# Four moves in the opening of a Fourier-mixing and feed-forward kernel on one core

## The chip, the core and the metric

The kernel runs on one core of a Trainium2 chip. A core has a matrix engine (TensorE, PE in the profile), a vector engine (VectorE, DVE), a scalar engine (ScalarE, ACT), a general engine (GpSimd, POOL) and a sync engine (SP) that here only starts transfers. The engines run their own instruction queues in order and wait for each other through semaphores. The metric is the time of one execution in device microseconds (us); lower is better. A group "PEld" in the profile is the loading of weights into TensorE, which overlaps its matmuls.

## What is computed

The reference, cut to what matters:

```python
# x: (8, 3008, 256), w_in: (256, 2048), w_out: (2048, 256), all float
X = np.fft.fft(x, axis=1)
X = np.fft.fft(X, axis=2)
x2 = X.real.astype(np.float32).reshape(8 * 3008, 256)
h = x2 @ w_in
g = h * (1.0 / (1.0 + np.exp(-1.702 * h)))
return (g @ w_out).astype(np.float32)
```

So eight batches are Fourier-transformed along the sequence (3008 = 47 x 64) and along the 256 columns, and the real part goes through a feed-forward layer of width 2048 with a sigmoid gelu. The weights arrive as 64-bit floats. [...] the kernel itself rounds them, in eight chunks (four of w_in, four of w_out), from the high and the low 32-bit word of each number.

## The kernel before

The kernel is a software pipeline over 8 batches x 6 half blocks x 8 pairs of hidden tiles. Step t of that pipeline computes the hidden activations of step t (`hidden`, `rows`, `activate`) and multiplies those of step t - 3 with w_out (`product`). The column transform is folded into w_in: a rounded chunk `wst` is multiplied by a small cosine and sine table (`fold_w`), and the results `wcs` are the weights of `hidden`. The sequence transform of batch b + 1 runs between the steps of batch b. What has nothing to hide behind is the opening: the sequence transform of batch 0 and the rounding and folding of the first weight chunks.

First the transform of batch 0. `xt` holds 32 slots of 256 columns, eight groups of four. `fold_first` adds and subtracts mirrored columns into a separate tile (`room`), with the two columns that have no mirror copied by GpSimd; `mix_first` multiplies pairs of slots into one bank of PSUM, and ScalarE copies the bank back into `xt`; `spill_first` writes it to DRAM (`Td`), from where `fill` reads it back in another layout.

```python
    def fold_first(g):

        t, e = xt[0:2 * NA, 4 * g:4 * g + 4, :], room[g][0:2 * NA]
        nc.gpsimd.tensor_copy(free(e, 0, [D, 4], [H, 2]), free(t, 0, [D, 4], [H, 2]))
        for at, op in ((1, ALU.add), (H + 1, ALU.subtract)):
            nc.vector.tensor_tensor(e[:, :, at:at + H - 1], t[:, :, 1:H], free(t, D - 1, [D, 4], [-1, H - 1]), op=op)

    def mix_first(i):

        ps, ns = bank("ps1"), (2 * i + 2, 2 * i + 1) if i < 7 else (0, 15)
        for at, n in enumerate(ns):
            for even in range(2):
                c0, c1 = (0, H + 1) if even else (H + 1, D)
                o = ps[:, at * D + c0:at * D + c1]
                for k, slot in enumerate((n, NJ - n if n else 16)):
                    rhs = room[slot // 4][:, slot % 4, c0:c1]
                    w = free(pair[:, even, slot], 0, [1, 128])
                    nc.tensor.matmul(o, lhsT=w, rhs=rhs, start=(k == 0), stop=(k == 1))
        nc.scalar.copy(xt[:, 30 - 2 * i:32 - 2 * i, :].rearrange("p j d -> p (j d)"), ps[:])

    def spill_first(lo, hi):
        for c, eng in enumerate((nc.sync, nc.scalar)):
            eng.dma_start(out=view(Td[0], (16 * c + lo - 16) * D, [NJ * D, NM], [1, (hi - lo) * D]),
                          in_=xt[NM * c:NM * c + NM, lo:hi, :].rearrange("p q d -> p (q d)"))
```

A chunk of the weights is rounded by three engines: a clamp on GpSimd, a square and two conversions of the low word on ScalarE (the square on VectorE for the first two chunks), three operations on VectorE, and an integer addition on GpSimd that ends it.

```python
    def bounds(key, first=False):


        hi, lo = raw[key][:, :, 1].bitcast(F32), raw[key][:, :, 0]
        g = sp.tile([128, 1024], F32, tag="s", bufs=3, name="g")
        m = cv.tile([128, 1024], F32, tag="m", bufs=2, name="m")
        r = cv.tile([128, 1024], U32, tag="r", bufs=2, name="r")
        nc.gpsimd.tensor_scalar(m[:], hi, scalar1=TOP, scalar2=-TOP, op0=ALU.min, op1=ALU.max)

        if first:
            nc.vector.tensor_tensor(g[:], hi, hi, op=ALU.mult)
        else:
            nc.scalar.activation(g[:], hi, ACTF.Square)
        nc.scalar.activation(r[:].bitcast(F32), lo, ACTF.Copy, scale=2.0 ** -29, bias=2.0 ** 23)
        nc.scalar.activation(r[:], r[:].bitcast(F32), ACTF.Copy, bias=-2.0 ** 23)
        pre[key] = g, m, r

    def rounded(outs, key):


    def rounded(outs, key):
        # ... (a = a tile of 128 x 1024 words; m is masked in place)
        dve.scalar_tensor_tensor(m[:], g[:], LOW * LOW, m[:], op0=ALU.is_ge, op1=ALU.mult)
        dve.tensor_scalar(a[:], bits, scalar1=3, scalar2=0x3FFFFFF8, op0=ALU.logical_shift_left, op1=ALU.bitwise_and)
        dve.scalar_tensor_tensor(a[:], bits, 0xC0000000, a[:], op0=ALU.bitwise_and, op1=ALU.bitwise_or)

        def finish():
            for out, part in outs(a[:], r[:]):
                nc.gpsimd.tensor_tensor(out.bitcast(U32), *part, op=ALU.add)
        return finish
```

`fold_w` with its last part, the `psf` matmuls that make the scalars `af2`:

```python
    def fold_w(n):
        for cs in range(2):
            ps = bank("psw")
            for i in range(2):
                nc.tensor.matmul(ps[:], lhsT=cd[:, i, cs, :], rhs=wst[n][:, i, :], start=(i == 0), stop=(i == 1))

            nc.scalar.copy(wcs[cs][:, n * 512:(n + 1) * 512].rearrange("p (f c) -> p f c", f=4),
                           free(ps[:], 0, [1, 4], [4, 128]))

        ps = bank("psf")
        for f in range(4 * n, 4 * n + 4):
            nc.tensor.matmul(ps[:, f:f + 1], lhsT=wcs[1][0:1, f * 128:f * 128 + 128], rhs=twos[:], start=True, stop=True)
        nc.scalar.copy(af2[:, 4 * n:4 * n + 4], ps[:, 4 * n:4 * n + 4])
```

The second stage of the sequence transform (`rotate` mends one column, `stage2` multiplies, VectorE transposes) and the first hidden tiles:

```python
    def rotate(b, a0=0, a1=NG, copy=None):

        col = t4t[b][:, a0:a1, H]
        ps = bank("psr")
        nc.tensor.matmul(ps[:, 0:a1 - a0], lhsT=rot, rhs=col, start=True, stop=True)
        (copy or nc.vector.tensor_copy)(col, ps[:, 0:a1 - a0])
    # ... stage2: 64 small matmuls t4 -> ps, then
        for cs in range(2):
            for u in range(NU):

                nc.vector.transpose(free(pq[:], cs * 512 + u * RUN, [256, 2], [NU * RUN, 4], [1, RUN]),
                                    free(ps[u][:], cs * 256, [128, 2], [32, 4], [1, 32]))
    # ... hidden(t): four matmuls wcs, pq -> pa, pb, then ScalarE copies pa to v
    # ... rows(t): VectorE, h = v + pb; dif = nb * af2 - pb (twice); h' = pa + dif
    # ... bank(): one of four PSUM banks in turn, for pa, pb, psw, psf, psn and warm
```

The opening itself, in program order:

```python
    nc.sync.dma_start(out=w0, in_=tab1[:, 0:n0 + 4])
    for part in ((0, 4), (28, 32), (4, 8), (24, 28), (8, 16), (16, 24)):
        load_first(*part)
    load_in(0, nc.sync)
    nc.sync.dma_start(out=small[:], in_=tab2)
    load_in(1, nc.sync)
    warm(7)

    nc.scalar.copy(af2[0:1, 0:1], ones[0:1, 0:1])
    matrices()
    for i, need in enumerate(((0, 7), (1,), (6,), (2,), (5,), (3,), (4,), ())):
        for g in need:
            fold_first(g)
        mix_first(i)
        if i == 2:
            specials()
        if i == 3:
            spill_first(24, 32)
            load_out(0, nc.sync)
        if i == 5:
            spill_first(20, 24)
    spill_first(16, 20)
    fill(0, 0, 4)
    load_in(2, nc.sync)
    load_out(1, nc.sync)
    for c in range(2):
        bounds(("in", c), True)
        round_in(c)
        finish_in(c)
    fold_w(0)
    warm(3)
    bounds(("out", 0))
    round_out(0)
    finish_out(0)
    rotate(0, 0, 4)
    stage2(0, 0)
    # ...
    ahead = [("in", 2), ("out", 1), ("in", 3), ("out", 2), ("out", 3)]
    at(0, bounds, ahead[0])
    for t, (kind, c) in enumerate(ahead):
        at(t, round_out if kind == "out" else round_in, c)
        if t + 1 < len(ahead):
            at(t, bounds, ahead[t + 1])
        at(t + 1, finish_out if kind == "out" else finish_in, c)
    early[0], early[2], early[4] = 1, 2, 3
    at(1, fill, 0, 4, NG)
    for t, load, c in ((0, load_in, 3), (1, load_out, 2), (2, load_out, 3)):
        at(t, load, c, nc.sync)
    # ...
    for t in range(n + LAG):
        if t < n:
            hidden(t)
        if t == 0:
            nyquist(0, 0)
        if t >= LAG:
            product(t - LAG)
        if t in early:
            fold_w(early[t])

        if 0 < t <= n:
            activate(t - 1)
            sums(t - 1, nc.gpsimd)
        sums(t - 2, nc.vector)
        if t < n:
            rows(t)
        if t >= LAG:
            combine(t - LAG)
        for fn, args in extra.get(t, ()):
            fn(*args)
```

`warm` is a run of matmuls whose results nobody reads.

## Time and profile before

| what | us |
|---|---|
| time, median of 3 runs | 1940.95 (1939.94 to 1941.74) |
| span of the profiled execution | 1946.2 |
| PE busy in the span | 1920.2 (99%) |
| PE busy from 100 us to 1900 us | 1800 of 1800 |
| VectorE, ScalarE, GpSimd busy in the span | 1415.1, 672.5, 767.1 |
| first matmul of `product` (line 520) | 81.68 |

Times in a profile count from the start of the span. Each row of the timeline has the start, the duration, the engine, the line of the kernel, the operation, its output and input, and the number of instructions merged; in brackets stands how long the engine sat idle before it and what released it. "PEclk" is the clock that TensorE was granted, as a share of full speed. A busy PE may be a slow PE: at half clock each matmul takes twice as long and still counts as busy. A float32 matmul appears as two records.

### The profile page before, as it was taken

To read this page: it belongs to the slowest core of one execution; us is meant where nothing else is said; L and a number is where in the kernel's file an instruction comes from. 1 tells how busy PE (TensorE), PEld (TensorE's weight loads), DVE (VectorE), ACT (ScalarE), POOL (GpSimd) and SP (SyncE) were. 2 spreads that over 40 slices of the span, in tenths; PEclk is the share of its full clock that TensorE was granted. 3 is DMA by queue.
4 is the path that set the end of the run, shared out by engine and by line. 5 is a ranking of instruction groups with operands and counts; after the bars stand their busy time and mean duration, and the time that the engine had idled before them with its cause. 6 is when DMAs were issued, how large, how long until landed. Compare 5 with 4: busy or idle time off the path is not lost.

```text
span 1946.2 us, 29330 instructions
## 1 busy us (share of the span) xinstructions
PE 1920.2 (99%) x10722; PEld 1681.4 (86%) x10722; DVE 1415.1 (73%) x2935; ACT 672.5 (35%) x922; POOL 767.1 (39%) x1062
## 2 busy tenths in 40 slices
PE   7899999999999999999999999999999999999998
PEld 5598888988889888898888888898888988889887
DVE  5567777777768777777678777777777777777776
ACT  3533333333333333333333333333333333333332
POOL 4356323643235432453225622255223643233332
PEclk8899999999999999999999999999999999999999
DMA  8630352218202272034521263221721213202201
GB/s 252 178 56 11 82 86 17 49 43 123 17 12 49 54 112 18 11 58 68 89 17 37 33 107 50 28 49 42 107 31 14 18 43 60 17 12 26 18 12 22
DMA packets 144560, 103.54 MB, mean 53 GB/s; under 512 B 104706, under 2 KB 127522, under 8 KB 142944
## 3 DMA queue, kind: packets, MB, share of 16 engines
q1 hardware_dynamic: 143136, 100.62, 31.0%
q8 instruction: 85, 1.39, 0.3%
q10 hardware_dynamic: 1280, 1.05, 0.2%
q14 instruction: 59, 0.48, 0.1%
HBM read 58.38 MB, written 48.01 MB: 55 GB/s over the span
## 4 chain that ended last, share of the span: by engine, by line
PE 98%; ACT 1%; DVE 0%; DMA 0%; POOL 0%; issue 0%; SPq 0%; ACTq 0%; DVEq 0%
PE po L520 59%; PE pa L453 17%; PE pb L453 17%; PE ps L213 1%; PE ps L318 1%; PE psw L422 1%; PE ps L270 1%; DMA xt<-in_x_dram 0%; PE ps L217 0%; POOL first L256 0%; PE psf L429 0%; ACT g L365 0%; DVE m L377 0%; ACT wcs L424 0%; POOL wst L384 0%
## 5 line engine op out<-in xcount | busy, mean ns | idle before, releaser
L520 PE MATMUL po<-s,wo 128*128 128x256 f32 (+1 forms) x3008 | 758.7, 375 | 0.0
L494 POOL TENSOR_TENSOR s<-h 128x256 f32<-128x256 f32 (+1 forms) x376 | 270.6, 720 | 1100.0 <-ACT h L482 1033.2
L520 PE MATMUL po<-h,wo 128*128 128x256 f32 (+1 forms) x2384 | 689.5, 375 | 0.0
L520 PEld LDWEIGHTS po<-s,wo 128*128 128x128 f32 x3008 | 571.5, 190 | 64.5
L457 ACT COPY v<-pa 128x512 f32<-128x512 f32 (+1 forms) x384 | 222.0, 578 | 1072.0 <-PE pa L453 1072.0
L467 DVE TENSOR_TENSOR h<-v,pb 128x512 f32<-128x512 f32 (+1 forms) x384 | 258.9, 674 | 409.3 <-PE pb L453 403.7
L520 PEld LDWEIGHTS po<-h,wo 128*128 128x128 f32 x2384 | 453.0, 190 | 51.7
L482 ACT ACTIVATE h<-h 128x1024 f32<-128x1024 f32 (+1 forms) x384 | 400.8, 1044 | 17.6 <-DVE h L477 16.0
L453 PE MATMUL pa<-pq,wcs 128*128 128x256 f32 (+1 forms) x1536 | 394.2, 379 | 0.9 <-DVE pq L324 0.9
L453 PE MATMUL pb<-pq,wcs 128*128 128x256 f32 (+1 forms) x1536 | 388.4, 375 | 0.0
L470 DVE SCALAR_TENSOR_TENSOR dif<-nb,af,pb 128x256 f32<-128x256 f32 (+1 forms) x768 | 328.2, 469 | 1.9 <-ACT nb L336 1.9
L453 PEld LDWEIGHTS pa<-pq,wcs 128*128 128x128 f32 x1536 | 286.8, 190 | 47.2 <-issue 10.0
L453 PEld LDWEIGHTS pb<-pq,wcs 128*128 128x128 f32 x1536 | 292.4, 190 | 33.3
L495 POOL TENSOR_TENSOR s<-h 128x256 f32<-128x256 f32 (+1 forms) x376 | 276.9, 736 | 0.0
L477 DVE TENSOR_TENSOR h<-pa,dif 128x512 f32<-128x512 f32 (+1 forms) x448 | 265.5, 604 | 13.2
L498 DVE TENSOR_TENSOR s<-h,s 128x256 f32<-128x256 f32 (+1 forms) x376 | 200.4, 533 | 12.9
L497 DVE TENSOR_TENSOR s<-s,h 128x256 f32<-128x256 f32 (+1 forms) x376 | 178.1, 474 | 4.3 <-POOL s L494 4.3
L199 POOL TENSOR_TENSOR xt<-xt 111x510 f32<-111x510 f32 x56 | 73.4, 1312 | 4.4
L554 DVE TENSOR_TENSOR c<-u,po 128x256 f32<-128x256 f32 (+1 forms) x188 | 69.4, 410 | 1.6
L324 DVE STREAM_TRANSPOSE pq<-ps 128x256 f32<-128x256 f32 x96 | 34.6, 417 | 44.6 <-PE ps L318 44.6
L554 DVE TENSOR_TENSOR u<-u,po 128x256 f32<-128x256 f32 (+1 forms) x141 | 57.7, 409 | 9.9 <-ACT u L525 4.6
L537 DVE STREAM_TRANSPOSE os<-c 128x512 f32<-128x512 f32 x94 | 61.1, 687 | 0.1
(71 smaller groups left out, 520.0 us busy)
## 6 DMA issues: line engine op xcount, KB each, us to landing
out_dram<-os SPq DMA_DIRECT2D x284, 64.0 KB
Td<-xt SPq DMA_DIRECT2D x14, 768.0 KB
t<-Td SPq DMA_DIRECT2D x7, 1536.0 KB
xt<-in_x_dram SPq DMA_DIRECT2D x14, 512.0 KB
xt<-Xr SPq DMA_DIRECT2D x14, 512.0 KB
nb<-pq SPq DMA_DIRECT2D x23, 256.0 KB
out_dram<-os SPq DMA_DIRECT2D x96, 56.0 KB
Xr<-in_x_dram SPq DMA_DIRECT2D x7, 752.0 KB
```

The source lines that it names most:

```text
L453: nc.tensor.matmul(ps[:, i * 256:i * 256 + n], lhsT=wcs[cs][:, f * 128:(f + 1) * 128], rhs=pq[:, cs, ks], start=True, stop=True)
L457: nc.scalar.copy(two(v[:], n), two(pa[:], n))
L467: nc.vector.tensor_tensor(two(h[:], n), two(v[:], n), two(pb[:], n), op=ALU.add)
L470: nc.vector.scalar_tensor_tensor(dif[:, i * 256:i * 256 + n], nb[:, ks], af2[:, f:f + 1], pb[:, i * 256:i * 256 + n], op0=ALU.mult, op1=AL ...
L477: nc.vector.tensor_tensor(free(h[:], 512 + at + m - 1, [256, 2], [RUN, blocks], [-1, m]), *ins, op=ALU.add)
L482: nc.scalar.activation(g, g, ACTF.Gelu_apprx_sigmoid)
L494: eng.tensor_tensor(s1, a21, a22, op=ALU.add)
L495: eng.tensor_tensor(s3, a11, a21, op=ALU.subtract)
L497: eng.tensor_tensor(s2, s1, a11, op=ALU.subtract)
L498: eng.tensor_tensor(s4, a12, s2, op=ALU.subtract)
L520: nc.tensor.matmul(pot[q][:, i, :n], lhsT=lhs, rhs=rhs, start=(p == 0 and i == 0 and f == 0), stop=(p == NP - 1), skip_group_check=True)
L554: nc.vector.tensor_tensor(out_, i0, i1, op=how)
```

## The change

All of it lies in the opening, before the pipeline is full. It is meant to take waits out of the first transform, to start rounding and second stage sooner, and to give TensorE work while chunks are rounded.

- Even columns in place. `fold_first` writes the differences into a room of half the size and the sums back into `xt` itself, where the two columns without a mirror already stand. GpSimd's copies of these columns go away, and the even matmuls read `xt`.
- Outputs in rooms of their own. As `xt` is still read, ScalarE copies the mixed banks into `made`, four tiles of four slots, and each is spilled as soon as its two banks are there (four pairs of transfers instead of three). The last 16 slots of x are loaded in four parts rather than two.
- First weight chunk in halves. The low words of the first chunk are converted between the mixing steps, and clamp, high word and addition run on two halves of 512.
- Order. The second stage of the sequence transform (and `rotate`'s copy, now on ScalarE) comes before the folding of the second weight chunk; that is folded before the pipeline's first step, the third is rounded before it, and `psf` is taken out of `fold_w` and made a step later. The gelu table is the first that ScalarE loads. The transfers of w_out and of the rest of `Td` are issued in another order.

Core of the diff, cut where marked:

```diff
-        nc.gpsimd.tensor_copy(free(e, 0, [D, 4], [H, 2]), free(t, 0, [D, 4], [H, 2]))
-        for at, op in ((1, ALU.add), (H + 1, ALU.subtract)):
-            nc.vector.tensor_tensor(e[:, :, at:at + H - 1], t[:, :, 1:H], free(t, D - 1, [D, 4], [-1, H - 1]), op=op)
+        fwd, rev = t[:, :, 1:H], free(t, D - 1, [D, 4], [-1, H - 1])
+        nc.vector.tensor_tensor(e[:, :, 0:H - 1], fwd, rev, op=ALU.subtract)
+        nc.vector.tensor_tensor(fwd, fwd, rev, op=ALU.add)
 ...
-                    rhs = room[slot // 4][:, slot % 4, c0:c1]
+                    rhs = xt[:, slot, c0:c1] if even else room[slot // 4][:, slot % 4, 0:H - 1]
 ...
-        nc.scalar.copy(xt[:, 30 - 2 * i:32 - 2 * i, :].rearrange("p j d -> p (j d)"), ps[:])
-
-    def spill_first(lo, hi):
+        to = 2 - i % 2 * 2
+        nc.scalar.copy(made[i // 2][:, to:to + 2, :].rearrange("p j d -> p (j d)"), ps[:])
+
+    def spill_first(k):
         for c, eng in enumerate((nc.sync, nc.scalar)):
-            eng.dma_start(out=view(Td[0], (16 * c + lo - 16) * D, [NJ * D, NM], [1, (hi - lo) * D]),
-                          in_=xt[NM * c:NM * c + NM, lo:hi, :].rearrange("p q d -> p (q d)"))
+            eng.dma_start(out=view(Td[0], (16 * c + 12 - 4 * k) * D, [NJ * D, NM], [1, 4 * D]),
+                          in_=made[k][NM * c:NM * c + NM].rearrange("p q d -> p (q d)"))
 ...
+    def clamp(key, lo=0, n=1024):
+        nc.gpsimd.tensor_scalar(pre[key][1][:, lo:lo + n], raw[key][:, lo:lo + n, 1].bitcast(F32), scalar1=TOP, scalar2=-TOP,
+                                op0=ALU.min, op1=ALU.max)
+
+    def low_up(key, lo=0, n=1024):
+
+        nc.scalar.activation(pre[key][2][:, lo:lo + n].bitcast(F32), raw[key][:, lo:lo + n, 0], ACTF.Copy, scale=2.0 ** -29,
+                             bias=2.0 ** 23)
+
+    def low_down(key, lo=0, n=1024):
+        r = pre[key][2][:, lo:lo + n]
+        nc.scalar.activation(r, r.bitcast(F32), ACTF.Copy, bias=-2.0 ** 23)
+
+    def bounds(key):
+        prepare(key)
+        squares(key, nc.scalar)
+        clamp(key)
+        low_up(key)
+        low_down(key)
 ...
-    def fold_w(n):
+    def fold_w(n, between=()):
+        between = iter(between)
         for cs in range(2):
             ps = bank("psw")
             for i in range(2):
@@ -423,6 +440,11 @@
 
             nc.scalar.copy(wcs[cs][:, n * 512:(n + 1) * 512].rearrange("p (f c) -> p f c", f=4),
                            free(ps[:], 0, [1, 4], [4, 128]))
+            for fn, key in between:
+                fn(key)
+                break
+
+    def first_row(n):
 ...
-    for part in ((0, 4), (28, 32), (4, 8), (24, 28), (8, 16), (16, 24)):
+    for part in ((0, 4), (28, 32), (4, 8), (24, 28), (8, 12), (20, 24), (12, 16), (16, 20)):
 ...
-    nc.scalar.copy(af2[0:1, 0:1], ones[0:1, 0:1])
+    nc.scalar.activation(af2[0:1, 0:1], ones[0:1, 0:1], ACTF.Gelu_apprx_sigmoid)
     matrices()
+    in0, in1, out0, in2 = ("in", 0), ("in", 1), ("out", 0), ("in", 2)
+    prepare(in0)
     for i, need in enumerate(((0, 7), (1,), (6,), (2,), (5,), (3,), (4,), ())):
         for g in need:
             fold_first(g)
         mix_first(i)
+        if i % 2:
+            spill_first(i // 2)
         if i == 2:
             specials()
-        if i == 3:
-            spill_first(24, 32)
-            load_out(0, nc.sync)
-        if i == 5:
-            spill_first(20, 24)
-    spill_first(16, 20)
+
+        if i in (4, 5):
+            h0 = 512 * (i - 4)
+            low_up(in0, h0, 512)
+            low_down(in0, h0, 512)
+        if i == 6:
+            squares(in0, nc.vector)
+            for h0 in (0, 512):
+                clamp(in0, h0, 512)
+                high(in0, h0, 512)
+                finish_in(0, h0, 512)
+    load_out(0, nc.sync)
     fill(0, 0, 4)
     load_in(2, nc.sync)
+    fill(0, 4, NG)
     load_out(1, nc.sync)
-    for c in range(2):
-        bounds(("in", c), True)
-        round_in(c)
-        finish_in(c)
+    load_in(3, nc.sync)
+    prepare(in1)
+    squares(in1, nc.vector)
+    clamp(in1)
+    low_up(in1)
+    low_down(in1)
+    high(in1)
+    finish_in(1)
     fold_w(0)
+    prepare(out0)
+    squares(out0, nc.vector)
+    clamp(out0)
+    low_up(out0)
+    low_down(out0)
+    high(out0)
+    finish_out(0)
     warm(3)
-    bounds(("out", 0))
-    round_out(0)
-    finish_out(0)
-    rotate(0, 0, 4)
+    rotate(0, 0, 4, nc.scalar.copy)
     stage2(0, 0)
+    prepare(in2)
+    squares(in2, nc.scalar)
+    clamp(in2)
+    fold_w(1, ((low_up, in2), (low_down, in2)))
+    high(in2)
+    finish_in(2)
+    first_row(0)
 ...
-    ahead = [("in", 2), ("out", 1), ("in", 3), ("out", 2), ("out", 3)]
-    at(0, bounds, ahead[0])
-    for t, (kind, c) in enumerate(ahead):
-        at(t, round_out if kind == "out" else round_in, c)
-        if t + 1 < len(ahead):
-            at(t, bounds, ahead[t + 1])
-        at(t + 1, finish_out if kind == "out" else finish_in, c)
-    early[0], early[2], early[4] = 1, 2, 3
-    at(1, fill, 0, 4, NG)
-    for t, load, c in ((0, load_in, 3), (1, load_out, 2), (2, load_out, 3)):
-        at(t, load, c, nc.sync)
+    for t, key in (2, ("out", 1)), (3, ("in", 3)), (5, ("out", 2)), (6, ("out", 3)):
+        at(t, round_chunk, key)
+    early[2], early[4] = 2, 3
+    rows_at = {1: 1, 3: 2, 5: 3}
+    for t, c in ((0, 2), (1, 3)):
+        at(t, load_out, c, nc.sync)
 ...
+        if t in rows_at:
+            first_row(rows_at[t])
```

The function names above are those of the changed kernel: `low_up` and `low_down` are the two conversions on ScalarE, `high` the three operations on VectorE, `finish_in` and `finish_out` the additions on GpSimd.

## Prediction

> **What bounds the kernel now.** I read the page first. Its share row says that TensorE is busy in 99% of the span, and its slices say where it is not, and where its clock is low:
>
> ```profile
> PE 1920.2 (99%) x10722; PEld 1681.4 (86%) x10722; DVE 1415.1 (73%) x2935; ACT 672.5 (35%) x922; POOL 767.1 (39%) x1062
> ...
> PE   7899999999999999999999999999999999999998
> ...
> PEclk8899999999999999999999999999999999999999
> ```
>
> One slice is 48.7 us. Only the first two have gaps and a clock under 0.9. In the table of stages TensorE is busy for 1800 of the 1800 us from 100 to 1900, at clock 1.00. The diff leaves that work alone, so the time changes by what it moves the start of the dense part, and by nothing else. The chain that ended last, between 79 and 82 us, shows that start: the first `product` (line 520) follows `hidden` without a gap, and from there on the chain is TensorE.
>
> ```profile
> 71.60 6.61 PE psw L422 x8
> 78.23 0.60 ACT wcs L424
> 78.87 1.05 PE psf L429 x8
> 79.92 1.06 PE pa L453 x4
> 80.98 0.86 PE pb L453 x4
> ```
>
> What TensorE must have done by 81.7 us: eight mixes (128 records of 0.11 us, the fast ones of the timeline, 14.1), three `fold_w` (3.45 each as at 90.3 us, 10.4), three `psf` (1.05, 3.2), four `hidden` (1.72, 6.9), second stage, `rotate` and `psn` (2.5): 37 us at full clock. So some 44 us of the opening are idle time, half clock and empty `warm` matmuls (11.3). That is the most that could be won; it is 2.3% of the time, and a chain of loads and rounding has to fit in too.
>
> What holds TensorE in the opening, by the timeline. The transform: GpSimd's copy of two columns keeps the first mixes waiting.
>
> ```profile
> 8.69 4.61 POOL L256 COPY first<-xt 94x8 f32<-94x8 f32 x2 [1.18 <-DMA xt<-in_x_dram]
> ```
>
> One of these two copies took 4.48 us where the median of its group is 0.197. VectorE ran its folds back to back from 8.25 to 13.1 us, and the copy ended in VectorE's first pause. TensorE stood from 11.55 to 13.22 and then went on at half clock (28 records in 6.36 us) to 19.5. It finished the mixing at 30.1. The rounding: chunk 0 of w_in landed at 20.3 us (GpSimd's clamp waits for it until then), yet its low words are converted only at 31.1, after the last ScalarE copy of the mixing.
>
> ```profile
> 33.44 2.36 POOL L384 TENSOR_TENSOR wst<-a,r 128x1024 uint32<-128x1024 uint32 x1 [10.82 <-ACT r L367]
> 35.76 1.10 POOL L360 TENSOR_SCALAR m<-raw 128x1024 f32<-128x1024 f32 x1
> ```
>
> After it clamp (GpSimd), three operations (VectorE) and addition (GpSimd) of the next chunk follow one another. The second stage waits until 47.97 us for VectorE to copy one column (line 305), which stands in VectorE's queue behind the rounding of the first w_out chunk. Last, TensorE stands from 66.6 to 71.6 us, and twice it falls to half clock (about 50.4 to 60.4 and 70.7 to 77.5 us).
>
> **What the Trainium skill says.** "GPSIMD Engine Reference", section 8, Key points: GpSimd shares its SBUF interfaces with VectorE, with contention when VectorE has two SBUF inputs. The trace agrees: the starved copy, and a clamp of 2.28 us beside a VectorE product of 2.15, where they take 1.10 and 1.22 alone. The two together need about the sum. "TensorE: Matmul & The Clock Gate", Part 1: The HAM clock gate: an idle window of about 3.4 us halves the clock, about as much work restores it. Here the granted clock fell at about 33.1 us, 3 us after the last mix, and came back at 39.9, 4.1 us after the next matmul began. "DMA: Bandwidth & Descriptors", Anatomy of one DMA (told there for transfers that GpSimd starts): about 2 us are fixed, most of it the receipt of the write. Here the last spill was issued at 30.74 us, traffic ended near 34.5, and the `fill` that waits for it was issued at 36.05.
>
> **The change, part by part.** Loads and mixing. Loads land as before, x at 17.9 us. But the spills now start near 14.6 us on ScalarE's queue, beside the loads; two of these halves, 0.2 MB each, at the 260 to 410 GB/s that the windows show before 20 us, put w_in chunk 0 some 0.9 us later, at 21.2. Fold per group stays two VectorE operations of 0.67 us, and the copies are gone. Mixing starts when the second group is folded, near 10.3 us (before: 9.7, then two stops). With no stop over 1 us after `warm` the clock should stay full, so 8 x 1.76 us gives 24.4 us, not 30.1.
>
> Fill. The spills end later than the mixing, because DMA is the limit: loads and spills are 8.1 MB, which the old trace had moved by about 30.4 us; it ran half empty from 23 to 26 us, which the early spills fill, so I take 29.5. With 2 us of receipt the fill is issued at 31.5, not 36.05, and landed at 35.5 if it takes the 4 us that I read from the traffic after 36.05.
>
> Rounding, which I expect to be the new path. Halves cost half: VectorE 0.65 + 0.37 + 0.65 = 1.65 us, GpSimd addition 1.2, clamp 0.57. From 21.2: square and first clamp share the ports, 1.8 (23.0); high 24.6; addition 25.8; clamp 26.4; high 28.0; second addition, beside the square of chunk 1, 2.4 (30.4). So chunk 0 is ready at 30.4, not 35.8. Chunk 1: clamp 1.1, high 3.15, addition 2.36 beside another square, 3.6: 38.3. First w_out chunk: clamp 39.4, high 42.6, then the four transposes of the second stage on VectorE, 1.44: 44.0. Addition 45.1, clamp of w_in chunk 2 46.2, high 49.4.
>
> TensorE beside that: `fold_w` 0 until 34 to 36, `warm`, `rotate` and second stage done by about 39.5, `fold_w` 1 from 39.5 to 43, `psf`, first `hidden` 44.1 to 45.8, `psn` to 46.8, half of the second `hidden` to 47.7. Then a wait I expect to see: the next bank is freed by `rows(0)`, which stands on VectorE behind the rounding of chunk 2 and takes 49.4 to 51.6 (0.69 + 0.87 + 0.69). Nearly 4 us idle, so half clock for 4 us more. `hidden` 1 and 2 and one `psf` until 57.3, `fold_w` 2 until 60.8 (its chunk is ready at 51.8), `hidden` 3 until 62.5, `psf`, first `product` at 63.5. Before it was 81.7, with exactly the same work done: 18.2 us. One small thing more: at 93.9 to 95.6 us TensorE lost about 1 us before `psf` (0.42 busy in one microsecond), and `psf` now comes a step later, off that wait. Afterwards VectorE needs per step 2.25 for `rows` and 3.15 for a chunk, about 5.4 us, beside 5.2 to 8.6 of TensorE, so the dense part should hold. The gelu table, 1.28 us at 69.97 us, moves to the start beside an idle ScalarE and only shortens what was hidden. Sum: 18 to 19 us, and I take 1 off for what a hand count misses: 17, so 1924.
>
> **The rivals.** First, the rounding chain is slower than I count. It is a ping-pong of two engines on shared ports, and three squares on VectorE (one of them new) lie beside GpSimd additions. If each overlap starves GpSimd until VectorE pauses, as the copy at 8.69 did, `rows(0)` moves to 54 to 56 and the first product to 68: a gain of 13. For it speaks the 4.48 us copy, against it that clamp and square shared. Second, transfers: spills in four parts on two queues delay loads, and the fill sets the second stage. If chunk 0 landed at 24 and the fill at 40, the whole chain would move by 3: a gain of 15; the second stage alone has some 3 us of room, since its transposes wait for VectorE until 42.6. Third, the clock: if mixing again ran half its time at 0.5, it would end near 28, which the DMA limit of the fill nearly hides, but half clock between 28 and 36 and again after 48 could cost 3 to 4 us: a gain of 14. Fourth, the other way: VectorE needs no contention allowance (3 us less), and TensorE never falls to half clock at 51 (3 us less): a gain of 23. That the start moves but later steps give it back I hold unlikely, for PE is full and at clock 1.00 from 100 us on, and nothing there waits for the opening.
>
> **Range and chances.** Middle 1924. The rivals one by one give 1918 to 1928, two of the bad ones together about 1932; so 1917 to 1932. Faster by over 2% means 38.8 us, nearly all of the 44 us of loss: 0.01. Slower by over 2% would need the opening to last 120 us: 0.005.
>
> **What would show it.** The copies' line gone, mixing without stops and done near 24 to 25 us at full clock. Addition of chunk 0's second half ending near 30, not 36. The fill issued near 31 to 32. VectorE's transposes at about 43 and not 48.7. A TensorE gap before 52 us released by VectorE's `rows`, with a half clock after it. The first `product` at 63.5 us. It is wrong if the first product lies outside 58 to 71, if mixing still runs at half clock past 16 us, or if the dense part that follows has idle microseconds.

## The result and the profile after

| kernel | median us | lowest to highest | ratio to before, 95% |
|---|---|---|---|
| before | 1941.35 (4 runs) | 1939.94 to 1944.94 | |
| changed | 1934.97 (4 runs) | 1932.14 to 1936.30 | 0.9962 (0.9945 to 0.9980) |

The change made the kernel faster by 6.4 us (0.4%), where 17 were predicted; 1934.97 lies above the range of 1917 to 1932.

The page of the changed kernel, its share row and its slices (one slice is now 48.3 us), beside those shown of before:

```profile
PE 1914.2 (99%) x10722; PEld 1677.6 (87%) x10722; DVE 1414.6 (73%) x2937; ACT 670.7 (35%) x923; POOL 764.0 (40%) x1057
...
PE   8899999999999999999999999999999999999998
...
PEclk9899999999999999999999999999999999999999
```

TensorE has the same 10722 instructions and 6.0 us less of busy time; as the work is the same, that is half clock saved. The first slice is fuller and its clock higher, as hoped. But the second slice, 48.3 to 96.7 us, is still at 8 in both rows: the pipeline is running by then, and it still has a gap. The timeline of TensorE in the changed kernel shows it (the columns are those of before: start, duration, engine, line, operation, operands, merged records, and in brackets the idle time and its releaser; rows left out are marked):

```profile
62.75 3.72 PE L542 MATMUL po<-h,wo 128*128 128x256 f32 x16
66.31 1.03 PE L475 MATMUL pa<-pq,wcs 128*128 128x256 f32 x4
67.17 1.03 PE L475 MATMUL pb<-pq,wcs 128*128 128x256 f32 x4
68.03 3.62 PE L542 MATMUL po<-h,wo 128*128 128x256 f32 x16
75.62 6.35 PE L439 MATMUL psw<-wst,small 128*128 128x512 f32 x8 [3.97 <-POOL wst L412]
...
84.82 3.72 PE L542 MATMUL po<-h,wo 128*128 128x256 f32 x16
```

The first `product` starts at 62.75 us, close to the 63.5 of the prediction. After the second one TensorE stands for 4 us until GpSimd has added the words of w_in chunk 3, and then the fourth `fold_w` takes 6.35 us, where a full clock makes it 3.60: from 75 to 80 us the granted clock was 0.50. The third product starts at 84.82, which is 22.1 us after the first. In the trace of before the two stand 15.9 us apart (81.68 and 97.61). So 6.1 us were given back between the first and the third product. From the third product to the end of the span, the traces of all kernels in this study take 1848.4 to 1848.8 us; what differs lies ahead of it. (The timed figure is 1.8 us above the span of its trace in both kernels, so the two can be compared.)

That leaves a second riddle. By the two traces the spans differ by 12.9 us (1946.2 and 1933.3), by the timed runs 6.4. The experiments take up both.

### The profile page after: what moved, and what is told of

Same layout as the page of the kernel before. It is cut to its first block, busy times and chain, and to the rows that moved or that the text cites. A ratio compares the mean times of both kernels' runs of the same rounds, so it can differ in the third digit from the quotient of the medians.

```text
span 1933.3 us, 29337 instructions
## 1 busy us (share of the span) xinstructions
PE 1914.2 (99%) x10722; PEld 1677.6 (87%) x10722; DVE 1414.6 (73%) x2937; ACT 670.7 (35%) x923; POOL 764.0 (40%) x1057
## 4 chain that ended last, share of the span: by engine, by line
PE 96%; DVE 1%; DMA 1%; POOL 1%; issue 0%; ACT 0%; SPq 0%; POOLq 0%; DVEq 0%
PE po L542 59%; PE pa L475 17%; PE pb L475 17%; PE ps L213 1%; PE ps L320 1%; DMA raw<-in_moe_w_in_dram 1%; PE psw L439 1%; POOL wst L412 0%; DMA xt<-in_x_dram 0%; DVE m L398 0%; POOL m L371 0%; DVE a L400 0%; PE ps L217 0%; DVE a L399 0%; POOL wo L420 0%
## 5 line engine op out<-in xcount | busy, mean ns | idle before, releaser
L520 DVE TENSOR_TENSOR s<-h,s 128x256 f32<-128x256 f32 (+1 forms) x376 | 198.9, 529 | 12.9
```

Of the source, the lines that this page charges most:

```text
L520: eng.tensor_tensor(s4, a12, s2, op=ALU.subtract)
```

## The experiments

The main theory was that the fourth fold gives time back because its chunk is rounded too late; the rivals were that the lead at the first product had been overrated, and that single parts of the change (fold in place, halves, order of the second stage) brought little or did harm. The changed kernel and the three groups of experiments (1 to 4, 5 to 8, 9 to 12) were timed each beside runs of the kernel before, whose medians were 1941.35, 1941.22, 1941.90 and 1941.30 us; the ratios are to these. A difference between two of the kernels is one of medians of 4 or 5 runs, and one of 1 to 2 us lies within their spread.

**1. The kernel before, again.** No edit. Does the opening of before always look like the trace that the prediction was counted from?

> The kernel before, unchanged, traced a second time. The traced span of before was 1946.2 us, but its timed runs lie at 1940 to 1945. Theory S (the trace was a slow sample of the opening): a span of about 1939 to 1941 here with the first product at 75 to 77 us instead of 81.7, because half-clock phases fall elsewhere. Rival D (the dense part varies): first product again at 81 to 82 us, and the difference lies after 100 us. Time against before: same, within 2 us.

Thirteen runs gave a median of 1941.54, beside 1941.22 for 33 others of the same kernel on the same chip; ratio 1.0001 (0.9993 to 1.0010). The trace had a span of 1943.6 us, a first product at 78.94 and a third at 94.88: 2.7 us earlier than in the trace of the prediction, and still one of the long executions (1945.34). So the first trace was no fixed picture. The span and first product that theory S named were not met, but rival D fails: from the third product to the end it is 1848.7 us, as in the first trace. Runs 11 and 12 below take this up.

**2. Chunk 3 of w_in ahead of chunk 1 of w_out.** Only the order in which two chunks are rounded changes:

```diff
-    for t, key in (2, ("out", 1)), (3, ("in", 3)), (5, ("out", 2)), (6, ("out", 3)):
+    for t, key in (2, ("in", 3)), (3, ("out", 1)), (5, ("out", 2)), (6, ("out", 3)):
```

> The changed kernel with the two chunks of steps 2 and 3 exchanged: w_in chunk 3 is rounded in step 2, w_out chunk 1 in step 3. Theory Q (queue order: chunk 3 of w_in waits on GpSimd behind the addition of w_out chunk 1, and the third fold waits for it): first product stays at 62 to 64 us, the 4 us gap of TensorE at 71.7 to 75.6 and the half clock after it are gone, third product near 78.5 us instead of 84.8, and the time is about 6 us under the changed kernel, 1928 to 1930. Rival W: the wait only moves to the product that needs w_out chunk 1, third product at 83 us or later, time within 2 us of the changed kernel.

Measured 1926.69 (1925.75 to 1928.04), ratio 0.9924 (0.9910 to 0.9937): 8.3 us less than the changed kernel. TensorE's timeline of this kernel, the same stretch as above:

```profile
60.91 3.72 PE L542 MATMUL po<-h,wo 128*128 128x256 f32 x16
64.46 1.03 PE L475 MATMUL pa<-pq,wcs 128*128 128x256 f32 x4
65.33 1.03 PE L475 MATMUL pb<-pq,wcs 128*128 128x256 f32 x4
66.19 3.62 PE L542 MATMUL po<-h,wo 128*128 128x256 f32 x16
69.64 3.60 PE L439 MATMUL psw<-wst,small 128*128 128x512 f32 x8
...
76.10 3.72 PE L542 MATMUL po<-h,wo 128*128 128x256 f32 x16
```

The wait is gone, the fold runs at full clock, and first and third product are 15.2 us apart instead of 22.1. (The "third fold" of the expectation is this one, the fold of chunk 3.) The first product too comes 1.8 us earlier, 60.91 after 62.75: in this trace TensorE's clock did not fall at 53 us, as it did in that of the changed kernel. That is 8 us before the first of the squares that the edit moves, so this part may be chance; the rest, 6.9 us, is the wait and the half clock. The table of stages says the same for 70 to 80 us, first the changed kernel, then this one (the first columns are the stretch and its length, then busy time and instructions of PE, PEld, DVE, ACT and POOL; then TensorE's granted clock, the DMA share and GB/s):

```profile
70.00:80.00 10.00, 6.03 (x13) 2.96 (x12) 5.05 (x7) 0.59 (x2) 3.41 (x2) 0.71 0.85 256
```

```profile
70.00:80.00 10.00, 10.00 (x44) 7.31 (x43) 7.01 (x12) 6.37 (x9) 3.64 (x3) 1.00 0.78 242
```

GpSimd's timeline of this kernel gives the margin that the exchange makes. The addition of chunk 3 ends at 66.7 us, 2.9 us before the fold wants it, and the w_out addition, which has time, comes after it:

```profile
64.36 2.39 POOL L412 TENSOR_TENSOR wst<-a,r 128x1024 uint32<-128x1024 uint32 x1 [10.61 <-DVE a L400]
66.71 1.16 POOL L371 TENSOR_SCALAR m<-raw 128x1024 f32<-128x1024 f32 x1
71.26 2.48 POOL L420 TENSOR_TENSOR wo<-a,r 128x512 uint32<-128x512 uint32 x2 [3.40 <-DVE a L400]
```

**3. Both chunks a step earlier, order kept.** A rival reading was that it is the order of these two chunks that matters, and not how late the second is:

```diff
-    for t, key in (2, ("out", 1)), (3, ("in", 3)), (5, ("out", 2)), (6, ("out", 3)):
+    for t, key in (1, ("out", 1)), (2, ("in", 3)), (5, ("out", 2)), (6, ("out", 3)):
```

> The changed kernel with the same two chunks each one step earlier: w_out chunk 1 in step 1, w_in chunk 3 in step 2. Theory Q: no gap before the fourth fold, third product at 78 to 80 us, 5 to 7 us under the changed kernel; the first product may move later by up to 2 us, as VectorE then rounds before the third hidden step. Rival V (VectorE is the scarce engine before the first product): first product at 66 us or later and less than 3 us gained.

Measured 1927.67 (1926.27 to 1928.36), ratio 0.9926 (0.9914 to 0.9938): 7.3 us less than the changed kernel, and first and third product 15.2 us apart (61.03 and 76.22). Another way of having chunk 3 in time does the same, with the order kept, so lateness is the cause. Rival V's later first product did not come. These are also the steps at which the kernel before rounds the two chunks.

**4. The fold in place and the outputs in rooms of their own, alone.** The kernel before, with the changed `fold_first`, `mix_first`, `spill_first`, rooms and x loads in eight parts; nothing of the rounding changes. From the edit:

```diff
-        nc.gpsimd.tensor_copy(free(e, 0, [D, 4], [H, 2]), free(t, 0, [D, 4], [H, 2]))
...
+        nc.vector.tensor_tensor(e[:, :, 0:H - 1], fwd, rev, op=ALU.subtract)
+        nc.vector.tensor_tensor(fwd, fwd, rev, op=ALU.add)
...
+        if i % 2:
+            spill_first(i // 2)
         if i == 3:
-            spill_first(24, 32)
             load_out(0, nc.sync)
-        if i == 5:
-            spill_first(20, 24)
-    spill_first(16, 20)
```

> The kernel before with the transform part of the change alone: fold in place, outputs in rooms of their own, x in eight parts, four spills. Theory T (the mixing's end starts ScalarE's conversions and so the rounding): mixing ends near 25 instead of 30.1 us, the addition of the first chunk near 30.5 instead of 35.8, and all later steps move with it, first product about 5 us earlier, time 4 to 5 us under before. Rival R (the later chunks hang on loads and their own chain): mixing and first chunk earlier as said, but the first product moves by less than 2 us.

Measured 1939.21 in 21 runs (1937.71 to 1943.97), ratio 0.9988 (0.9981 to 0.9994): 2.0 us by the medians, less than the 4 to 5 of the theory. In its trace the mixing ends at 25.1 us and the first addition at 30.8, as hoped, but the first product stands at 73.27. That is 8.4 us ahead of the trace of the prediction, and only 0.5 ahead of the traces of runs 11 and 12, where the mixing ends at 27 us; against these it is rival R that holds.

**5. The changed kernel with the old transform.** The reverse: `fold_first` with GpSimd's copies, `mix_first`, spills in three pairs, rooms and loads in six parts as before.

```diff
+        nc.gpsimd.tensor_copy(free(e, 0, [D, 4], [H, 2]), free(t, 0, [D, 4], [H, 2]))
...
-        if i % 2:
-            spill_first(i // 2)
+        if i == 3:
+            spill_first(24, 32)
+        if i == 5:
+            spill_first(20, 24)
+        if i == 7:
+            spill_first(16, 20)
```

> The changed kernel with its transform part undone: GpSimd copies, outputs back into the tile of x, x in six parts, three spills. Theory C (rounding sets the start, mixing and fill run beside it): mixing ends at 27 to 31 us instead of 25.5, the fill is issued 3 to 5 us later, and yet the first product moves by under 1.5 us from 62.75; time within 2 us of the changed kernel. Rival T (the transform's stop was what held the opening): first product 4 to 6 us later, time 4 to 6 us more than the changed kernel.

Measured 1934.99 (1933.64 to 1936.38), ratio 0.9962 (0.9950 to 0.9975): equal to the changed kernel to 0.02 us, though a difference of up to 2 us would not show in so few runs. Its mixing ended near 26.9 us instead of 25.5 and its `fill` was issued at 31.46 instead of 29.89, but the first product stands at 63.36, 0.6 later, and the third at 84.53, 0.3 earlier. The slow copy is there again, in the forms of the tile `xt` (line, what, shortest, median and longest in ns, first and last start in us):

```profile
L257 POOL COPY first<-xt x3: 192/197/3022, 7.2 to 11.6; 94x8 f32<-94x8 f32 x3
```

One copy took 3.02 us, and the first product moved by only 0.6 us. Inside the changed kernel the first chunk's rounding, and not the mixing, sets the start for the most part: what the later mixing still did was to hold the low words of that chunk, so that its first addition came at 25.79 us, 0.6 after that of the changed kernel, although the chunk had landed 0.7 earlier.

**6. The first chunk whole.** The halves are undone, everything else stays:

```diff
-        if i in (4, 5):
-            h0 = 512 * (i - 4)
-            low_up(in0, h0, 512)
-            low_down(in0, h0, 512)
+        if i == 5:
+            low_up(in0)
+            low_down(in0)
         if i == 6:
             squares(in0, nc.vector)
-            for h0 in (0, 512):
-                clamp(in0, h0, 512)
-                high(in0, h0, 512)
-                finish_in(0, h0, 512)
+            clamp(in0)
+            high(in0)
+            finish_in(0)
```

> The changed kernel with the first chunk rounded whole instead of in halves. Theory P (ping-pong: with the clamp of the second half queued behind the addition of the first, halves cost a round trip): the last addition of this chunk ends near 30 instead of 31.2 us, first product 0.5 to 1.5 us earlier, time the same or 1 us less than the changed kernel. Rival H (halves overlap as they are meant to): the last addition 1 to 2 us later and the first product with it.

Measured 1933.00 (1931.53 to 1934.24), ratio 0.9952 (0.9940 to 0.9965): 2.0 us less than with halves. GpSimd's timeline of the changed kernel, from the landing of the first chunk on:

```profile
21.39 1.72 POOL L371 TENSOR_SCALAR m<-raw 128x512 f32<-128x512 f32 x1 [6.32 <-DMA raw<-in_moe_w_in_dram]
25.18 1.26 POOL L412 TENSOR_TENSOR wst<-a,r 128x512 uint32<-128x512 uint32 x1 [2.06 <-DVE a L400]
26.41 0.65 POOL L371 TENSOR_SCALAR m<-raw 128x512 f32<-128x512 f32 x1
29.12 2.10 POOL L412 TENSOR_TENSOR wst<-a,r 128x512 uint32<-128x512 uint32 x1 [2.06 <-DVE a L400]
31.20 1.09 POOL L371 TENSOR_SCALAR m<-raw 128x1024 f32<-128x1024 f32 x1
35.68 3.21 POOL L412 TENSOR_TENSOR wst<-a,r 128x1024 uint32<-128x1024 uint32 x1 [3.40 <-DVE a L400]
```

And with the chunk whole:

```profile
20.13 2.18 POOL L371 TENSOR_SCALAR m<-raw 128x1024 f32<-128x1024 f32 x1 [5.81 <-DMA raw<-in_moe_w_in_dram]
25.70 3.19 POOL L412 TENSOR_TENSOR wst<-a,r 128x1024 uint32<-128x1024 uint32 x1 [3.40 <-DVE a L400]
28.86 1.11 POOL L371 TENSOR_SCALAR m<-raw 128x1024 f32<-128x1024 f32 x1
33.37 3.21 POOL L412 TENSOR_TENSOR wst<-a,r 128x1024 uint32<-128x1024 uint32 x1 [3.40 <-DVE a L400]
```

In halves the second clamp stands in GpSimd's queue behind the first addition, so it cannot start before 26.41, and VectorE has nothing to do from 25.1 until it is done. The two engines take turns twice instead of once, and wait 2.06 us for each other each time. The chunk is done at 31.2 us in halves and at 28.9 whole; of these 2.3 us, 1.3 come from an earlier landing in the second trace. From landing to last addition it is 9.8 us in halves and 8.8 whole, and the same in the traces of experiments 2 and 9, where the chunk lands at 21.3 and 21.5 us. So halves cost 1.0 us in the chunk. The medians differ by 2.0 here and by 1.4 from experiment 2 to 9; both differences have the same sign, though in both the ranges of the runs overlap. The wait at the fourth fold stays: 4.02 us, ending at 71.66.

**7. The second stage after the second fold.** The part of the change that moves it ahead is undone:

```diff
-    warm(3)
-    rotate(0, 0, 4, nc.scalar.copy)
-    stage2(0, 0)
     prepare(in2)
...
     fold_w(1, ((low_up, in2), (low_down, in2)))
+    warm(3)
+    rotate(0, 0, 4, nc.scalar.copy)
+    stage2(0, 0)
```

> The changed kernel with the second stage put back behind the second fold. Theory C (VectorE's rounding and not TensorE's order sets the release of the banks): second fold near 39 to 42.5 us, transposes near 45, the first rows on VectorE still at 50 to 51 us, first product within 1 us of 62.75. Rival O (the order of stage two is worth what it moves): first product 2 to 4 us later.

Measured 1934.30 (1933.45 to 1935.91), ratio 0.9960 (0.9946 to 0.9973): no difference that these runs can tell. The dates of theory C for transposes and rows were missed by 1 to 3 us, its date of the first product was met. The second fold moved up from 40.46 to 38.37 us, the transposes moved down from 43.18 to 47.60 and `rows(0)` from 50.18 to 52.05, and the first product stayed (62.93).

**8. Clamps ahead of additions, squares on ScalarE.** On top of experiment 2, to see what the opening still holds. Every clamp of the opening goes ahead of the additions in GpSimd's queue, and the squares of two chunks go from VectorE to ScalarE:

```diff
+            clamp(in0, 0, 512)
+            clamp(in0, 512, 512)
+            prepare(in1)
+            clamp(in1)
             for h0 in (0, 512):
-                clamp(in0, h0, 512)
                 high(in0, h0, 512)
...
-    squares(in1, nc.vector)
-    clamp(in1)
+    squares(in1, nc.scalar)
...
     clamp(out0)
+    finish_in(1)
+    fold_w(0)
+    squares(out0, nc.scalar)
...
+    clamp(in2)
     finish_out(0)
```

> The changed kernel with w_in chunk 3 rounded before w_out chunk 1, and in the opening each chunk's clamp issued ahead of the addition of the chunk before, the squares of the second and third chunk on ScalarE. Theory C: the first rows on VectorE begin at 44 to 47 us instead of 50.2, first product at 56 to 59 us, time 3 to 5 us under the kernel with only the two chunks exchanged, so 1922 to 1924. Rival L (loads: the clamps ahead wait for their raw chunks and hold up the additions): first rows later than 48 us, under 2 us gained.

Measured 1924.49 (1922.19 to 1925.50), ratio 0.9907 (0.9893 to 0.9920): 2.2 us less than experiment 2, short of the 3 to 5 of theory C. `rows(0)` starts at 47.08 us instead of 50.18 in the changed kernel. But rival L came true in part: the clamps wait for their data, until 25.98, 33.22 and 37.25 us, and the addition of the first half, whose operand VectorE had ready at 25.1, starts at 27.11 behind the first of them. As clamps and squares were moved together, what each brought is not shown.

**9. Whole first chunk and chunk 3 first.** Experiments 2 and 6 together; the edit is the sum of theirs.

> The changed kernel with both findings: the first chunk rounded whole, and w_in chunk 3 before w_out chunk 1. If the two gains are separate steps of one chain they add: first product at 58 to 59.5 us, third at 73.5 to 75, time 1924 to 1925.5. If the exchange already took what the halves cost, first product at 61 and 1926 to 1927.

Measured 1925.30 (1924.14 to 1925.89), ratio 0.9914 (0.9900 to 0.9928). In the medians the two gains add: 9.7 us below the changed kernel, where 8.3 and 2.0 would make 10.3. The spans of the traces of experiments 2 and 6 would have made 12.3, with the early landing and the clock at 53 us counted in; here the first product stands at 60.09 and the third at 75.28.

**10. On top of 9, squares of two chunks on ScalarE.**

```diff
-    squares(in1, nc.vector)
+    squares(in1, nc.scalar)
...
-    squares(out0, nc.vector)
+    squares(out0, nc.scalar)
```

> As the kernel with both findings, and the squares of w_in chunk 1 and w_out chunk 0 on ScalarE instead of VectorE. Theory X (the shared ports: a VectorE square beside a GpSimd addition stretches it): the two additions of 3.2 us each take 2.4 (2.3 to 2.5), the first rows on VectorE begin 1.4 to 2 us earlier, time 1 to 2 us less. Rival A (ScalarE is then late with the squares or the low words): additions 2.4 us, yet the first rows not earlier than 47.5 us, time within 1 us.

Measured 1924.47 (1924.23 to 1926.92), ratio 0.9914 (0.9901 to 0.9928). GpSimd's additions, with VectorE no longer squaring beside them, in this kernel:

```profile
26.52 2.37 POOL L412 TENSOR_TENSOR wst<-a,r 128x1024 uint32<-128x1024 uint32 x1 [3.40 <-DVE a L400]
...
33.37 2.34 POOL L412 TENSOR_TENSOR wst<-a,r 128x1024 uint32<-128x1024 uint32 x1 [3.39 <-ACT wcs L441]
```

They take 2.37 and 2.34 us, where they took 3.19 and 3.22 in experiment 9. So it was the squares on VectorE that made these additions long. `rows(0)` comes 2.1 us earlier (47.09 after 49.21) and the first product 1.5 (58.58 after 60.09), but the medians differ by 0.8, which these runs do not tell apart.

Experiments 8 and 10 give the shortest times, about 10.5 us below the changed kernel and 17 below the kernel before.

**11 and 12. The kernel before, two single executions.** No edit.

> The kernel before, one more look, for the spread of its opening. Theory S: if its span is near 1939 us, TensorE is at half clock for about 15 us of the opening instead of 31, and the third product starts near 90.5 us instead of 97.6; the span minus that start is 1848.5 us as in all traces so far. Rival D: the span minus the start of the third product differs by over 1 us.

> As the look before it: span minus start of the third product 1848.5 us within 0.3 (theory S), with any difference of the spans found in half-clock phases before 90 us; rival D: over 1 us of difference after the third product.

Times 1940.07 and 1940.09, both spans 1938.3 us, the first product at 73.73 and 73.71, the third at 89.67 and 89.64. The stages of the first of them, at the two places where the trace of the prediction was at half clock:

```profile
10.00:20.00 10.00, 8.79 (x69) 7.79 (x67) 5.97 (x11) 2.34 (x4) 5.70 (x11) 1.00 1.01 271
...
50.00:60.00 10.00, 8.60 (x33) 5.36 (x32) 4.53 (x7) 6.06 (x9) 0.31 (x1) 1.00 0.18 43
```

The same stages in the trace that the prediction was counted from:

```profile
10.00:20.00 10.00, 7.59 (x40) 7.30 (x39) 6.48 (x12) 1.17 (x2) 6.81 (x11) 0.66 1.02 290
...
50.00:60.00 10.00, 10.00 (x17) 4.37 (x16) 2.42 (x5) 1.76 (x3) 2.63 (x3) 0.51 0.32 108
```

The copies of GpSimd stretch in both (two of them 3.31 us together here, 4.61 in the trace of the prediction), but TensorE stood 0.48 us for them here and kept its clock, and there 1.67 us and lost it. The second place is clearer, for the stops ahead of it are the same. First run 11, then the trace of the prediction:

```profile
45.63 0.67 PE L318 MATMUL ps<-t,small 64*32 64x128 f32 x32 [1.19 <-DVE t L305]
47.23 1.13 PE L453 MATMUL pa<-pq,wcs 128*128 128x256 f32 x4 [0.92 <-DVE pq L324]
```

```profile
47.97 0.67 PE L318 MATMUL ps<-t,small 64*32 64x128 f32 x32 [1.19 <-DVE t L305]
49.56 1.50 PE L453 MATMUL pa<-pq,wcs 128*128 128x256 f32 x4 [0.92 <-DVE pq L324]
```

After the same two stops the clock fell at 50.4 us in one and stayed full in the other; between 50 and 60 us TensorE did 33 matmul records in 8.6 us or 17 in 10. Experiment 1 parts the two places: there the clock held over the mixing and fell at the second, and its first product, 78.94, is 2.7 us ahead of the first trace and 5.2 behind run 11. So the half clock at the second place is worth some 5 us. Most timed runs of the kernel before lie at 1939.5 to 1942.8, and 6 of 33 at 1945 to 1946; the execution that was profiled first took 1947.98.

## Why the prediction was wrong

**Up to the first product its dates were right.** Measured against the steps it named: w_in chunk 0 landed at 21.3 us (said 21.2), mixing ended at 25.5 at full clock (24.4), the chunk's second addition ended at 31.2 (30.4), the `fill` was issued at 29.9 (31.5), VectorE's transposes came at 43.2 (42.6), `rows(0)` at 50.2 (49.4), and the first product at 62.75 (63.5). The wait before 52 us that it foretold is there, released by VectorE's `dif` of `rows`, shorter (1.35 us) than the "Nearly 4 us" and with the half clock behind it (1.45 and 1.91 us for the two `hidden` halves that take 1.03 at full clock):

```profile
51.70 1.05 PE L451 MATMUL psf<-twos,wcs 1*128 1x1 f32 x8 [1.35 <-DVE dif L492]
53.00 1.45 PE L475 MATMUL pa<-pq,wcs 128*128 128x256 f32 x4 [0.25 <-ACT af L452]
54.24 1.91 PE L475 MATMUL pb<-pq,wcs 128*128 128x256 f32 x4
```

**The step that failed is "so the dense part should hold"**, and with it "That the start moves but later steps give it back I hold unlikely". They rested on sums per step, VectorE's 5.4 us beside TensorE's 5.2 to 8.6, and on the table of stages from 100 us on. The fourth fold, due at 71.65 us, lies before that, and it depends on a date, not on a sum. The sum counted VectorE alone, while a chunk passes through ScalarE, VectorE and GpSimd in turn. The prediction's own last sign of being wrong, idle microseconds behind the first product, came true here. The chain of the changed kernel (start, duration, what), from the gelu ahead of the first square to that fold, pieces of up to 0.1 us left out:

```profile
60.63 1.06 ACT h L504
61.69 1.02 ACT g L366
62.81 1.24 DVE m L398
...
67.41 1.27 POOL wo L420
68.69 1.12 POOL m L371
69.83 1.24 DVE m L398
71.09 0.70 DVE a L399
71.82 1.24 DVE a L400
73.22 2.35 POOL wst L412
75.62 6.35 PE psw L439 x8
```

Two chunks stand in line. The square of w_out chunk 1 is queued on ScalarE behind the copies of the third fold and a gelu and starts at 61.69 us; its addition ends at 68.7. Only then does GpSimd clamp chunk 3 of w_in, whose rounding lasts until 75.6. Each takes 7 us from first operation to addition, 13.9 together; the fold wants the second one 10 us after 61.69. The code shows it: the kernel before rounds these chunks at steps 1 and 2, with their clamps a step ahead of that, the changed kernel at steps 2 and 3, while the fold stays at step 4. TensorE's idle 3.97 us and 2.75 of half clock in the fold (6.35 less 3.60) make 6.7; experiments 2 and 3 took the wait away in two ways, and the medians fell by 8.3 and 7.3. "TensorE: Matmul & The Clock Gate" in the Trainium skill, Part 1: The HAM clock gate, says that an idle window of about 3.4 us halves the clock. Here the stop of 3.97 us did halve it, but the granted clock fell at 74.2, 2.5 us after the last matmul, and it was full again at 81.0, 5.4 us after the fold began.

**The second step that failed is "Before it was 81.7, with exactly the same work done: 18.2 us."** The 81.7 was read in one trace, of an execution that took 1947.98 us, and the gain counted from it was taken off a median of 1940.95. Against that trace the lead at the first product is 18.9 us (81.68 less 62.75). Less the 6.6 by which the traced execution exceeds the median of 1941.35, and less the 6.1 that are given back by the fourth fold, 6.2 remain; measured are 6.4, with an interval of 3.9 to 10.7. Runs 11 and 12 (1940.07 and 1940.09, some 1.2 us below the median) show it directly: there the first product stands at 73.7, the lead is 11.0 us, and 4.9 remain at the third product (89.67 and 84.82). Counting forward instead of by difference would have avoided it: first product 63.5, plus 15.9 to the third, plus 1848.6 for the rest, plus 1.8 between span and timed figure makes 1929.8. The 5.2 us from there to the measured 1934.97 are in the main the give-back of 6.1, less the 0.75 us by which the first product came sooner.

**The parts.** The transform, with the mixing at half clock and the starved copy, was the loss that the prediction read most clearly in the trace. It brings 2.0 us alone (experiment 4) and nothing that shows in the changed kernel (experiment 5), since there the rounding sets the start, as the prediction itself says ("which I expect to be the new path"). The halves, counted as "Halves cost half", cost 1 us in the trace and 1.4 to 2.0 in the medians: the count has the second clamp behind the first addition, but it leaves out what the whole chunk would have taken, which is less. The order of the second stage makes no difference that shows. `psf`, moved off a wait that was counted as about 1 us, brings 0.75: first and third product stand 15.94 us apart in run 11 and 15.19 in experiments 2 and 3.

Where the lead of 11.0 us over run 11 lies, the traces tell. The first fold ends at 39.2 there and at 36.8 in the changed kernel, so 2.5 us are won up to it and 8.5 between it and the first product. Of these, 6.8 lie at the third fold, first in run 11, then in the changed kernel:

```profile
64.25 5.99 PE L422 MATMUL psw<-wst,small 128*128 128x512 f32 x8 [4.98 <-DVE dif L470]
```

```profile
55.95 4.17 PE L439 MATMUL psw<-wst,small 128*128 128x512 f32 x8
```

All four traces of before have this stop, of 4.97 to 5.00 us, and so has experiment 4; the changed kernel and experiments 5 to 7, each without one of its parts, do not. In run 11 VectorE's `rows` come late because a copy from ScalarE comes late, and that copy stands behind the squares and conversions of two chunks (55.7 to 62.1 us). In the changed kernel chunk 2 stands ahead of the first step in program order. So the stop belongs neither to the transform nor to the halves nor to the place of the second stage, and by elimination to rounding that begins earlier and is woven between the other work; but no experiment made that part alone, so this much is argued and not shown.

**The rivals.** Slower rounding by shared ports was real in size (3.2 us for 2.35 in the additions, as the prediction allowed for) and did not move the first product beyond the count. The transfers did not delay it: chunk 0 landed on the count, and the `fill` was issued 1.6 us ahead of it. The clock did fall where the third rival feared it (0.67 as the mean of 30 to 40 us, and again from 53), and still the first product came on the count; what came on top, a stop and half clock at the fourth fold, no rival looked for. All four rivals varied the date of the first product and held everything behind it fixed, so the range could not hold the answer.

## What to carry to other kernels

When a change pulls the start of a pipeline forward, look for the first steps whose inputs have a date of their own, and count for each when its operand is ready and when it is wanted; that busy time per step fits says nothing of two operands in one queue. Count the time forward from an absolute chain, and set the traced execution beside the timed ones before a difference is taken from it: here the trace of before was 7 us above the median. When a piece of work is cut in halves between two engines that serve their queues in order, look where the second half's first operation stands: here it stood behind the first half's last, and halves cost 1 us. Queued ahead (experiment 8) it does not wait for that addition, but a clamp of the next chunk, queued ahead too, then held the addition up until its data had come.

## What the runs showed of the hardware

The opening of one and the same program varied by 8 us: spans of 1946.2, 1943.6, 1938.3 and 1938.3 us, with first products at 81.68, 78.94, 73.73 and 73.71, and everything from the third product on equal within 0.2 us. Behind most of it lies the granted clock: after two stops of TensorE of 1.19 and 0.92 us (1.20 and 0.93 in experiment 1) it fell to half in two of these executions, for 10 us, and stayed full in the other two. Both stops are much shorter than the window of 3.4 us cited above, so a stop need not be that long. What decides between the two outcomes is not shown, nor why GpSimd's copies take 1.86 to 4.61 us for the same two from run to run.

A GpSimd addition of 128x1024 words takes 2.35 us alone and 3.2 beside a VectorE square, one of 128x512 1.26 and 2.10. "GPSIMD Engine Reference" in the Trainium skill, section 8, Key points, names contention between the two engines for VectorE work with two SBUF inputs; the traces agree, and experiment 10, which gives the squares to ScalarE, brings 2.37 and 2.34 back.
